# A new order for the later loads and for the work of batches 0 and 1 in a fused attention and feed-forward kernel

## The chip, the cores and the metric

One Trainium2 chip, one core. The metric is device time in microseconds (us). Each execution is listed with its span (first to last instruction) and the mean clock that TensorE was granted. A run of a program on one core carries the state "fast" unless it is more than 1.5% above the fastest of its kernel. The runs were spread over several chips; kernels are compared only with runs of the kernel before on the same chip.

Names used below: PE is TensorE's matmul stream, PEld its weight loads, DVE is VectorE, ACT is ScalarE, POOL is GpSimd, SPq is the queue that issues the loads.

## The reference, cut to what matters

```python
# q, k, v: (8 batches, 8 heads, 576 positions, 64); w_in 512x2048, w_out 2048x512
q_s = softmax(q, axis=-1)                # over the 64 features
k_s = softmax(k, axis=2)                 # over the 576 positions
kv  = einsum('bhsd,bhse->bhde', k_s, v)
x   = einsum('bhsd,bhde->bhse', q_s, kv) # reshaped to 4608 tokens x 512
h   = x @ w_in
out = (h * sigmoid(beta * h)) @ w_out
```

## The kernel before

The 512 main positions of each batch are one chunk of tokens; the last 64 positions of all batches form a ninth. From batch 2 on a loop does the work. Batches 0 and 1, while the weights still arrive, are written out by hand: the program is one long list of small steps, and the place of a step in the list is its place in its engine's queue. The steps that matter here:

```python
def hpe(c, j, kts, tag="h"):      # PE: h block j of chunk c, the 128-row parts kts of w_in
    ...
    nc.tensor.matmul(h[:], w_unit(j, kt), x_of(c)[:, kt, :], start=(kt == 0), stop=(kt == KT - 1))
def th_act(c, j): ...             # ACT: tanh of h
def g_dve(c, j): ...              # DVE: g = (tanh + 1) * h
def mm_b(c, j, sts=None): ...     # PE: 4 matmuls, acc += g x w_out block j
def w_cast(kind, blk, half, eng)  # f32 weights to bf16 on the engine named: G POOL, A ACT, V DVE
def vz_cast(b, j, eng, m=1, part=None)   # f32 v of batch b, head pair j to bf16
def kz_exp(b, j): ...             # ACT: exp of k
def q_exp(b, s) / q_sum / q_mul   # ACT: exp of q; DVE: its sums; DVE: scale by them
def tpe(b, j, tag) / q_ev         # PE: transpose scaled q into a PSUM bank; copy it out
def kvz_mm(b, j) / kvz_norm       # PE: 18 small matmuls k x v; DVE: normalise
def xpe(c, j, tag) / xev          # PE: x = q (kv); copy it out
def warm(n, tag):                 # PE: n matmuls whose result nobody reads
    t = ps.tile([P, 512], F32, tag=bank(tag), bufs=1, name=f"warm{warm_n[0]}")
    ...
```

The loads are issued in this order (cut: the first are batch 0's q, k and v, whose order the change leaves alone):

```python
    w_load("in", 0, 0)
    w_load("in", 0, 3)
    w_load("in", 0, 1)
    w_load("in", 0, 2)
    ...
    w_load("out", 1)
    load_kv(v_st, v, 1, "v_st", [0])
    w_load("in", 3, 0)
    w_load("in", 3, 1)
    load_q(1, 2, 0)
    w_load("out", 2)
    load_q(1, 2, 1)
    load_kv(v_st, v, 1, "v_st", [1])
    load_kv(k_st, k, 1, "k_st", [0])
    ...
```

And three places of the list of work (cuts marked):

```python
    warm(18, tag="b0")
    ...
    warm(13, tag="acc2")
    tpe(0, 0, "acc3")
    ...
    vz_cast(0, 3, G, part=0)
    vz_cast(0, 3, A, part=1)
    kvz_mm(0, 2, "acc1", 2)
    xev(0, 0, A)
    kvz_mm(0, 3)
    ...                                   # 31 us: 
    vz_cast(1, 0, A, part=1)
    th_act(0, 10)
    mm_b(0, 6)
    w_cast("in", 3, 1, A)
    ...                                   # 40 us:
    tpe(1, 0, "b0")
    tpe(1, 1, "b1")
    q_ev(1, 0, A)
    kvz_mm(1, 0, "b3", 2)
    g_dve(0, 14)
    kvz_mm(1, 1)
    q_ev(1, 1, A)
    tpe(1, 3, "b0")
    ...
    kvz_mm(1, 3, "b1", 1)
    vz_cast(1, 2, G, part=0)
    mm_b(0, 14)
    vz_cast(1, 2, A, part=1)
    kvz_norm(1, 3)
    xev(1, 0, A)
    kvz_mm(1, 2, "b0", 1)
    mm_b(0, 15)
```

The softmax here doesn't subtract the row's maximum and nothing guards it: scores larger than these inputs give would overflow.

## Time and profile before

| | before |
|---|---|
| median of 3 runs | 284.43 us (284.4 to 284.81) |
| span of the profiled run | 282.9 us |
| PE busy | 275.2 us, 97% |
| granted clock | 1.000 |

From the page of the kernel before (span, busy time by engine, the clock by fortieths of the span in tenths of full speed, and the chain of work that ended last):

```profile
span 282.9 us, 4278 instructions
...
PE 275.2 (97%) x1653; PEld 130.1 (46%) x1681; DVE 176.5 (62%) x274; ACT 164.9 (58%) x243; POOL 39.6 (14%) x60
...
PEclk9999999999999999999999999999999999999999
...
PE 93%; DMA 3%; SPq 1%; POOL 1%; issue 1%; ACT 0%
```

PE is the bound: it is busy nearly always, at full clock, and the chain that ended last is made of it. So one reads where PE pauses. The timeline of the kernel before, PE alone (start, duration, engine, line, operation, output and inputs, how many merged; in brackets the idle time of the engine ahead of it and what ended it):

```profile
10.51 0.61 PE L273 MATMUL tp<-identity,eq 128*128 128x128 bf16 x8 [0.83 <-DVE eq L243]
...
13.93 0.48 PE L292 MATMUL kv<-va,ek 64*64 64x65 bf16 x18 [0.73 <-POOL va L161]
...
16.30 5.65 PE L425 MATMUL h<-xT,w_in_b 128*128 128x512 bf16 x25
...
39.70 0.61 PE L273 MATMUL tp<-identity,eq 128*128 128x128 bf16 x8
...
45.18 0.48 PE L292 MATMUL kv<-va,ek 64*64 64x65 bf16 x18
...
50.34 1.89 PE L473 MATMUL acc<-w_out_b,g 128*128 128x512 bf16 x8
```

The marks are four: the first transpose of batch 0 (10.51), the start of the long run of w_in matmuls (16.30), the first transpose of batch 1 (39.70) and the first acc matmul of batch 1 (50.34). Two pauses stand in brackets: 0.83 us for DVE's scaled q and 0.73 us for POOL's v cast. A duration of a merged line includes the drain of its last matmul, so pauses of a tenth show only by comparing starts: the 18 kv matmuls at 45.18 start at least 0.1 us after the acc matmuls ahead of them could have ended.

What came before the v cast is in the chain of waits of the kernel before (start, duration, what):

```profile
3.99 8.52 DMA v_st<-in_v_dram
...
12.56 1.31 POOL va L161
13.88 1.13 POOL w_in_b L161 x2
```

The last v load lands at 12.51 us and POOL's cast follows until 13.87.

Waits tell when loads landed. POOL in the timeline of the kernel before, stretches 22 to 33 us and 33 to 46 us:

```profile
28.94 1.04 POOL L161 CAST w_in_b<-w_in 128x1024 bf16<-128x1024 f32 x1 [0.89 <-DMA w_in<-in_moe_w_in_dram]
```

```profile
34.37 1.04 POOL L161 CAST w_out_b<-w_out 128x1024 bf16<-128x1024 f32 x1 [4.39 <-DMA w_out<-in_moe_w_out_dram]
```

Half 0 of block 3 of w_in was waited for until 28.94 us, block 2 of w_out until 34.37. And ACT, same kernel, 19 to 33 us:

```profile
30.57 0.43 ACT L159 CAST va<-v_st 128x256 bf16<-128x256 f32 x1
...
31.45 1.06 ACT L159 CAST w_in_b<-w_in 128x1024 bf16<-128x1024 f32 x1
32.39 1.08 ACT L226 ACTIVATE eq<-q_st 128x1024 bf16<-128x1024 f32 x1
```

ACT casts part of v and the other half of w_in 3 before it starts the exp of batch 1's q at 32.39 us.

### The profile page before, as it was taken

The numbers are of one execution on the slowest core, as the hardware profiler recorded it, in microseconds if no ns is written. First come the engines' busy times: TensorE is split into PE (matmuls) and PEld (weight loads), VectorE is DVE, ScalarE is ACT, GpSimd is POOL, SyncE is SP. The second block draws the span as 40 slices with busy tenths as digits, with TensorE's granted clock in tenths as the row PEclk, the third lists the DMA queues.
The fourth block names the chain that finished last, engine by engine and source line by source line (L and its number), as shares of the span: only waits on it lengthen the run. The fifth ranks groups of instructions, "written<-read, shape, count | busy, mean of one in ns | idle before, by whom it ended". The sixth has DMA issues, their size and how long they took to land.

```text
span 282.9 us, 4278 instructions
## 1 busy us (share of the span) xinstructions
PE 275.2 (97%) x1653; PEld 130.1 (46%) x1681; DVE 176.5 (62%) x274; ACT 164.9 (58%) x243; POOL 39.6 (14%) x60
## 2 busy tenths in 40 slices
PE   8799999999999999999999999999999999999995
PEld 3444454444444544444444444444445444445543
DVE  2864586975487547845785468655964595454361
ACT  2874987954496348644873568346935563554451
POOL 1565235220030003000300030000300000000000
PEclk9999999999999999999999999999999999999999
DMA  7999999929930993099407941599354033005003
GB/s 231 392 393 395 380 392 312 292 44 290 225 151 12 271 272 155 0 227 315 163 5 177 307 158 65 114 233 234 128 88 137 1 148 62 14 0 148 0 2 148
DMA packets 54868, 50.09 MB, mean 177 GB/s; under 512 B 26296, under 2 KB 47040, under 8 KB 54848
## 3 DMA queue, kind: packets, MB, share of 16 engines
q1 hardware_dynamic: 54704, 49.69, 58.7%
q8 instruction: 13, 0.21, 0.3%
q10 hardware_dynamic: 144, 0.13, 0.1%
q14 instruction: 7, 0.06, 0.1%
HBM read 36.71 MB, written 9.44 MB: 163 GB/s over the span
## 4 chain that ended last, share of the span: by engine, by line
PE 93%; DMA 3%; SPq 1%; POOL 1%; issue 1%; ACT 0%
PE h L425 44%; PE acc L473 42%; DMA v_st<-in_v_dram 3%; PE x L373 2%; PE kv L333 2%; PE acc L465 1%; PE kv L292 1%; SPq L122 1%; POOL va L161 0%; POOL w_in_b L161 0%; PE tp L273 0%; PE x L377 0%; SPq L119 0%; SPq L593 0%; SPq L96 0%
## 5 line engine op out<-in xcount | busy, mean ns | idle before, releaser
L435 ACT ACTIVATE th<-h,beta_t 128x512 bf16<-128x512 f32 x144 | 98.2, 688 | 93.4 <-PE h L425 87.2
L439 DVE SCALAR_TENSOR_TENSOR g<-th,h 128x512 bf16<-128x512 bf16 x144 | 97.7, 683 | 84.6 <-ACT th L435 82.7
L425 PE MATMUL h<-xT,w_in_b 128*128 128x512 bf16 x560 | 142.4, 379 | 1.0
L473 PE MATMUL acc<-w_out_b,g 128*128 128x512 bf16 x548 | 138.8, 379 | 0.5 <-issue 0.2
L425 PEld LDWEIGHTS <-w_in_b 128*128 128x128 bf16 x576 | 55.6, 98 | 64.4 <-POOL w_in_b L161 0.4
L473 PEld LDWEIGHTS <-g 128*128 128x128 bf16 x560 | 54.5, 98 | 65.6 <-DVE g L439 0.5
L161 POOL CAST va<-v_st 128x2048 bf16<-128x2048 f32 (+2 forms) x14 | 16.9, 1207 | 149.7 <-DMA v_st<-in_v_dram 149.4
L237 DVE TENSOR_REDUCE rq<-eq 128x16 f32<-128x1024 bf16 x18 | 21.9, 1216 | 7.6 <-ACT eq L226 7.6
L243 DVE TENSOR_TENSOR eq<-eq,rq 128x1024 bf16<-128x1024 bf16 x18 | 22.3, 1239 | 0.1
L226 ACT ACTIVATE eq<-q_st 128x1024 bf16<-128x1024 f32 x16 | 16.1, 1049 | 4.5 <-DMA q_st<-in_q_dram 4.5
L159 ACT CAST xT<-x 128x512 bf16<-128x512 f32 x18 | 10.6, 588 | 6.6 <-PE x L373 5.8
L161 DVE COPY o<-acc 128x512 f32<-128x512 f32 (+1 forms) x19 | 12.1, 670 | 3.4 <-PE acc L473 3.2
L159 ACT COPY o<-acc 128x512 f32<-128x512 f32 (+1 forms) x18 | 9.6, 576 | 7.0 <-PE acc L473 2.9
L161 DVE CAST xT<-x 128x512 bf16<-128x512 f32 x18 | 12.3, 685 | 0.9 <-PE x L373 0.9
L180 ACT ACTIVATE ek<-k_st 128x1024 bf16<-128x1024 f32 x12 | 12.6, 1047 | 0.0
L373 PE MATMUL x<-qsT,kvp 128*128 128x512 bf16 x32 | 11.6, 379 | 0.1
L546 PE MATMUL warm<-kvp 128*128 128x512 bf16 x31 | 8.5, 442 | 1.2 <-DVE kvp L626 1.2
L161 POOL CAST w_in_b<-w_in 128x512 bf16<-128x512 f32 (+1 forms) x12 | 7.5, 650 | 3.0 <-DMA w_in<-in_moe_w_in_dram 2.9
L161 POOL CAST w_out_b<-w_out 128x1024 bf16<-128x1024 f32 x4 | 5.0, 1248 | 7.5 <-DMA w_out<-in_moe_w_out_dram 7.5
L546 PEld LDWEIGHTS <-kvp 128*128 128x128 bf16 x31 | 3.3, 111 | 5.8 <-issue 2.2
L173 ACT ACTIVATE ek<-k_st 128x576 bf16<-128x576 f32 x8 | 5.2, 686 | 1.0 <-DMA k_st<-in_k_dram 1.0
L333 PEld LDWEIGHTS <-ek 128*64 128x64 bf16 x192 | 4.1, 111 | 2.5 <-ACT th L435 2.5
(45 smaller groups left out, 84.6 us busy)
## 6 DMA issues: line engine op xcount, KB each, us to landing
q_st<-in_q_dram SPq DMA_DIRECT2D x7, 1024.0 KB, 6.6
out_dram<-o SPq DMA_DIRECT2D x14, 512.0 KB, 3.4
k_st<-in_k_dram SPq DMA_DIRECT2D x6, 1024.0 KB, 9.5
v_st<-in_v_dram SPq DMA_DIRECT2D x6, 1024.0 KB, 10.6
w_in<-in_moe_w_in_dram SPq DMA_DIRECT2D x6, 512.0 KB, 9.4
v_st<-in_v_dram SPq DMA_DIRECT2D x8, 288.0 KB, 8.5
w_out<-in_moe_w_out_dram SPq DMA_DIRECT2D x4, 512.0 KB, 9.3
w_out<-in_moe_w_out_dram SPq DMA_DIRECT2D x2, 1024.0 KB, 11.2
```

The costliest lines, as they stand in the source:

```text
L159: eng.copy(dst, src)
L161: eng.tensor_copy(dst, src)
L180: nc.scalar.activation(ek[b][:, :, h, :].rearrange("p i h d -> p h i d"), k_st[b][:, h, 0 : R * D].rearrange("p h (i d) -> p h i d", i=R), ...
L226: nc.scalar.activation(eq[b][:, :, s * m : (s + 1) * m, :].rearrange("p i h d -> p h i d"), q_st[b][:, s * m : (s + 1) * m, :].rearrange(" ...
L237: nc.vector.tensor_reduce(rq[b][:, 0, :, h], eq[b][:, :, h, :], axis=AX.X, op=ALU.add)
L243: eng.tensor_tensor(eq[b][:, :, h, :], eq[b][:, :, h, :], rq[b][:, 1, :, h].unsqueeze(3).to_broadcast((P, R, m, D)), ALU.mult,)
L373: nc.tensor.matmul(t[:], kvp[:, c, j, :], qsT[c][:, :, j, :])
L425: nc.tensor.matmul(h[:], w_unit(j, kt), x_of(c)[:, kt, :], start=(kt == 0), stop=(kt == KT - 1),)
L435: nc.scalar.activation(th[:], h_of[c, j][:], ACTF.Tanh, scale=beta_t[:, j : j + 1])
L439: nc.vector.scalar_tensor_tensor(out=g[:], in0=th_of.pop((c, j))[:], scalar=1.0, in1=h_of[c, j][:], op0=ALU.add, op1=ALU.mult)
L473: nc.tensor.matmul(acc[st][:], g[:, ds(st * P, P)], w_out_b[:, j, :], start=(j == 0), stop=(j == NJ - 1),)
L546: nc.tensor.matmul(t[:], kvp[:, B - 1, 0, :], kvp[:, B - 1, :, :].rearrange("p j r -> p (j r)"))
```

## The change

Its words: same loads of batch 0, other order of later loads and of the work of batches 0 and 1 on all engines, worked out for other landing times. No arithmetic is added or removed other than five warm-up matmuls. The core of the diff (cut; bank names that only follow are left out):

```diff
-    HB, AB = ["b3", "b0"], ["b1", "b2"]
+    HB, AB = ["b0", "b1"], ["b2", "b3"]
...
     w_load("in", 0, 0)
-    w_load("in", 0, 3)
     w_load("in", 0, 1)
     w_load("in", 0, 2)
+    w_load("in", 0, 3)
...
     w_load("out", 1)
-    load_kv(v_st, v, 1, "v_st", [0])
+    w_load("in", 3, 1)
     w_load("in", 3, 0)
-    w_load("in", 3, 1)
     load_q(1, 2, 0)
     w_load("out", 2)
     load_q(1, 2, 1)
     load_kv(v_st, v, 1, "v_st", [1])
     load_kv(k_st, k, 1, "k_st", [0])
+    load_kv(v_st, v, 1, "v_st", [0])
     load_kv(k_st, k, 1, "k_st", [1])
     w_load("out", 3, 0)
+    w_load("out", 3, 1)
+    load_kv(k_st, k, 1, "k_st", [2])
+    load_kv(v_st, v, 1, "v_st", [3])
     load_kv(k_st, k, 1, "k_st", [3])
-    w_load("out", 3, 1)
-    load_kv(v_st, v, 1, "v_st", [3])
-    load_kv(k_st, k, 1, "k_st", [2])
...
-    warm(13, tag="acc2")
+    warm(18, tag="acc2")
...                                   # h6 before h7, h9 before h8, h7 after h4 (cut)
...                                   # casts between engines
-    w_castk(0, 2, G)
+    w_castk(0, 2, A)
-    w_cast("out", 0, 1, G)
+    w_cast("out", 0, 1, A)
-    w_castk(2, 2, G)
-    w_castk(2, 3, G)
+    w_castk(2, 2, A)
+    w_castk(2, 3, A)
-    w_cast("in", 3, 1, A)
+    w_cast("in", 3, 1, G)
-    w_cast("out", 3, 0, G)
+    w_cast("out", 3, 0, A)
-    w_cast("out", 3, 1, A)
+    w_cast("out", 3, 1, G)
...                                   # batch 1's attention, as it stands after
     tpe(1, 0, "b0")
     tpe(1, 1, "b1")
+    kvz_mm(1, 0, "b2", 2)
+    q_ev(1, 1, V)
+    kvz_mm(1, 1)
     q_ev(1, 0, A)
+    tpe(1, 3, "b1")
+    kvz_norm(1, 0, 2)
+    tpe(1, 2, "b3")
...
     mm_b(0, 14)
     vz_cast(1, 2, A, part=1)
+    vz_cast(1, 2, G, part=0)
+    kvz_mm(1, 3, "b0", 1)
+    kvz_mm(1, 2, "b1", 1)
     kvz_norm(1, 3)
     mm_b(0, 15)
```

More of the change, by code (lines that the diff above doesn't have):

```diff
@@ L666 @@
     tpe(0, 2, "b3")
-    w_castk(0, 3, G)
+    w_castk(0, 1, G)
     q_ev(0, 3, A)
@@ L671 @@
     xpe(0, 1, "acc3")
-    hpe(0, 2, [0], "b1")
+    hpe(0, 1, [0], "b1")
     q_ev(0, 2, A)
-    w_castk(0, 1, G)
-    hpe(0, 1, [0], "b2")
+    hpe(0, 2, [0], "b2")
     xev(0, 1, V)
     hpe(0, 0, [0], "acc0")
+    w_castk(0, 2, A)
     xpe(0, 3, "acc2")
-    w_castk(0, 2, G)
+    w_castk(0, 3, G)
     xpe(0, 2, "acc1")
     xev(0, 3, V)
+    hpe(0, 0, [1])
+    xev(0, 2, A)
     hpe(0, 1, [1])
-    xev(0, 2, A)
-    hpe(0, 0, [1])
     hpe(0, 3, [1])
@@ L704 @@
     g_dve(0, 1)
-    hpe(0, 6, [0], "b1")
+    hpe(0, 6, [0], "b2")
     hpe(0, 5, [2])
@@ L708 @@
     hpe(0, 5, [3])
-    hpe(0, 7, [0], "b2")
+    hpe(0, 7, [0], "b1")
     th_act(0, 0)
@@ L712 @@
     g_dve(0, 3)
+    hpe(0, 6, [2])
+    hpe(0, 6, [3])
+    th_act(0, 5)
     w_cast("out", 0, 0, G)
     hpe(0, 7, [1])
+    g_dve(0, 0)
     hpe(0, 7, [2])
-    th_act(0, 5)
-    hpe(0, 6, [2])
-    g_dve(0, 0)
-    hpe(0, 6, [3])
-    hpe(0, 7, [3])
+    hpe(0, 4, [0], "b0")
+    th_act(0, 6)
     g_dve(0, 5)
-    th_act(0, 6)
-    hpe(0, 4, [0], "b0")
-    w_cast("out", 0, 1, G)
+    hpe(0, 4, [1])
+    hpe(0, 4, [2])
     mm_b(0, 0)
-    th_act(0, 7)
+    w_cast("out", 0, 1, A)
     g_dve(0, 6)
     mm_b(0, 1)
-    g_dve(0, 7)
     w_castk(2, 0, G)
@@ L733 @@
     mm_b(0, 3)
-    w_castk(2, 2, G)
-    w_castk(2, 3, G)
-    hpe(0, 4, [1])
-    hpe(0, 4, [2])
+    w_castk(2, 2, A)
+    w_castk(2, 3, A)
     hpe(0, 4, [3])
-    hpe(0, 8, [0, 1, 2, 3], "b1")
+    hpe(0, 7, [3])
     th_act(0, 4)
     hpe(0, 9, [0, 1, 2, 3], "b2")
+    th_act(0, 7)
     g_dve(0, 4)
-    th_act(0, 8)
+    hpe(0, 8, [0, 1, 2, 3], "b3")
+    th_act(0, 9)
+    g_dve(0, 7)
     w_cast("out", 1, 0, A)
     hpe(0, 11, [0, 1, 2, 3], "b0")
-    g_dve(0, 8)
-    vz_cast(1, 0, G, part=0)
-    hpe(0, 10, [0, 1, 2, 3], "b1")
-    th_act(0, 9)
-    th_act(0, 11)
-    w_cast("in", 3, 0, G)
-    g_dve(0, 9)
+    g_dve(0, 9)
+    hpe(0, 10, [0, 1, 2, 3], "b1")
+    th_act(0, 8)
+    w_cast("in", 3, 1, G)
+    th_act(0, 11)
+    g_dve(0, 8)
     mm_b(0, 4)
@@ L755 @@
     g_dve(0, 11)
+    w_cast("in", 3, 0, G)
     mm_b(0, 5)
-    vz_cast(1, 0, A, part=1)
     th_act(0, 10)
     mm_b(0, 6)
-    w_cast("in", 3, 1, A)
     g_dve(0, 10)
-    mm_b(0, 7)
     q_exp(1, 0)
@@ L767 @@
     th_act(0, 13)
-    hpe(0, 14, [0, 1, 2, 3], "b2")
-    w_cast("out", 2, 0, A)
-    w_cast("out", 2, 1, G)
-    g_dve(0, 13)
-    hpe(0, 15, [0, 1, 2, 3], "b3")
-    th_act(0, 12)
+    mm_b(0, 7)
+    th_act(0, 12)
+    g_dve(0, 13)
+    w_cast("out", 2, 1, G)
+    w_cast("out", 2, 0, A)
+    hpe(0, 14, [0, 1, 2, 3], "b2")
     q_mul(1, 0)
+    hpe(0, 15, [0, 1, 2, 3], "b0")
     q_exp(1, 1)
+    g_dve(0, 12)
     mm_b(0, 8)
-    g_dve(0, 12)
     vz_cast(1, 1, G)
     th_act(0, 14)
-    mm_b(0, 9)
@@ L781 @@
     q_sum(1, 1)
     th_act(0, 15)
+    mm_b(0, 9)
+    kz_exp(1, 0)
+    vz_cast(1, 0, G, part=0)
     mm_b(0, 10)
-    kz_exp(1, 0)
     g_dve(0, 15)
+    vz_cast(1, 0, A, part=1)
+    kz_exp(1, 1)
+    g_dve(0, 14)
     mm_b(0, 11)
-    kz_exp(1, 1)
     q_mul(1, 1)
-    w_cast("out", 3, 0, G)
     tpe(1, 0, "b0")
+    w_cast("out", 3, 0, A)
     tpe(1, 1, "b1")
+    kvz_mm(1, 0, "b2", 2)
+    q_ev(1, 1, V)
+    kvz_mm(1, 1)
     q_ev(1, 0, A)
-    kvz_mm(1, 0, "b3", 2)
-    g_dve(0, 14)
-    kvz_mm(1, 1)
@@ L796 @@
-    q_ev(1, 1, A)
-    tpe(1, 3, "b0")
-    kz_exp(1, 3)
-    kvz_norm(1, 0, 2)
-    mm_b(0, 12)
-    w_cast("out", 3, 1, A)
-    tpe(1, 2, "b1")
-    xpe(1, 1, "b2")
-    vz_cast(1, 3, G, part=0)
-    q_ev(1, 2, V)
-    xpe(1, 0, "b3")
-    vz_cast(1, 3, A, part=1)
-    mm_b(0, 13)
-    xev(1, 1, V)
-    q_ev(1, 3, A)
-    kz_exp(1, 2)
-    kvz_mm(1, 3, "b1", 1)
-    vz_cast(1, 2, G, part=0)
+    tpe(1, 3, "b1")
+    kvz_norm(1, 0, 2)
+    tpe(1, 2, "b3")
+    w_cast("out", 3, 1, G)
+    mm_b(0, 12)
@@ L814 @@
+    q_ev(1, 2, A)
+    q_ev(1, 3, V)
+    kz_exp(1, 2)
+    xpe(1, 1, "b0")
+    xpe(1, 0, "b1")
+    xev(1, 1, V)
+    mm_b(0, 13)
+    vz_cast(1, 3, A, part=1)
+    vz_cast(1, 3, G, part=0)
+    xev(1, 0, A)
+    kz_exp(1, 3)
     mm_b(0, 14)
     vz_cast(1, 2, A, part=1)
+    vz_cast(1, 2, G, part=0)
+    kvz_mm(1, 3, "b0", 1)
+    kvz_mm(1, 2, "b1", 1)
     kvz_norm(1, 3)
-    xev(1, 0, A)
-    kvz_mm(1, 2, "b0", 1)
     mm_b(0, 15)
     kvz_norm(1, 2)
-    xpe(1, 3, "b1")
+    xpe(1, 3, "b0")
@@ L822 @@
     store(0, 0)
-    xpe(1, 2, "b0")
+    hpe(1, 0, [0], "b2")
     xev(1, 3, V)
-    hpe(1, 0, [0], "b2")
     hpe(1, 0, [1])
+    xpe(1, 2, "b1")
+    hpe(1, 1, [0], "b3")
+    store(0, 1)
     xev(1, 2, A)
-    hpe(1, 2, [0], "b3")
-    store(0, 1)
+    hpe(1, 1, [1])
+    hpe(1, 2, [0], "b0")
     hpe(1, 2, [1])
-    hpe(1, 1, [0], "b1")
     hpe(1, 0, [2])
+    store(0, 2)
     hpe(1, 0, [3])
-    store(0, 2)
-    hpe(1, 1, [1])
     hpe(1, 1, [2])
+    store(0, 3)
     th_act(1, 0)
-    store(0, 3)
@@ L839 @@
     hpe(1, 1, [3])
     hpe(1, 2, [2])
+    hpe(1, 2, [3])
     th_act(1, 1)
-    hpe(1, 2, [3])
+    hpe(1, 3, [0], "b1")
     g_dve(1, 0)
-    hpe(1, 3, [0], "b0")
     hpe(1, 3, [1])
+    hpe(1, 3, [2])
     th_act(1, 2)
-    hpe(1, 3, [2])
+    hpe(1, 3, [3])
     g_dve(1, 1)
-    hpe(1, 3, [3])
     mm_b(1, 0)
```

## The prediction

> **What bounds the kernel now.** TensorE. The page gives PE 275.2 of 282.9 us busy (97%), clock 1.00; the chain that ended last is 93% PE. The stage table has PE busy 33.72 of 34.04 us between 16.3 and 50.34 us. By hand: 145 matmuls of 512 columns at a pitch of 0.216 us (16 take 3.45 us), 16 transposes at 0.067 and 72 kv matmuls at 0.02 make 33.8 us. The Trainium skill ("TensorE: Matmul & The Clock Gate", Part 1) gives 215.7 ns per warm 512-column matmul; the trace agrees. So the reordered stretch holds some 0.2 us of stalls to win. Before 16 us PE waits 0.83 us for the first scaled q and 0.73 us for the v cast (chain: v load landed at 12.51 us, GpSimd cast until 13.88). The loads behind both are untouched.
>
> **What changes.** No arithmetic is removed. Added: 5 warm-up matmuls (1.1 us), which fill the 0.83 us hole and delay the first transpose by 0.1 to 0.2 us; the v wait absorbs that. Moved: casts between GpSimd and ScalarE; h6 before h7, h9 before h8, h7 after h4; PSUM banks (a consistent renaming); batch 1's first v load (288 KB), to seven loads later.
>
> **Loads.** By the slices the queues run full at about 390 GB/s until 44 us, so landings are running sums of sizes. Before (GpSimd's waits): v1[0] 27.6, w_in 3 28.9 and 30.3, w_out 2 34.4, w_out 3 39.4 and 41.5, last v piece 43.7 us. After, estimated: w_in 3 28.2/29.5, w_out 2 33.6, v1[0] 37.2, w_out 3 39.3/40.7, last piece 43.7. Nothing lands after its use.
>
> **Where stalls may appear,** from queues added up with trace durations (tanh 0.64 back to back, ScalarE cast 1.04, g 0.64, DVE sum and reciprocal 1.45, scale 1.2):
> 1. From 25.9 us ScalarE has five tanh and two w_out casts before the second half of w_out 1 is ready, about 31.2 us; PE wants it at about 31.1: 0.1 to 0.4 us.
> 2. DVE ends batch 1's second q scale at about 40.9 us, then evicts transpose 1 (0.42 us) before transpose 3 can reuse its bank: PE waits 0.2 to 0.4 us. Before, ScalarE did that copy and PE did not wait.
> 3. ScalarE's last exp and cast of batch 1 end at about 44.9/45.3 us, just when PE asks: 0 to 0.3 us; in exchange the short waits of before (0.4 us in all, 43.8 to 45.8) shrink.
> Net: batch 1's first acc matmul starts at 50.4 to 50.9 us against 50.34. From there both kernels are the same PE-limited stream; what is lost stays lost.
>
> **Prediction.** About +0.35 us: **284.8 us**, 8 in 10 between **284.2 and 286.2**. Faster by over 2% 0.01, within 2% 0.97, slower by over 2% 0.02. A gain beyond 0.3 us is not there to be had.
>
> **What would show it.** Right: first transpose within 0.3 us of 10.5; w_in matmuls running without pause from near 16.3; short waits (below 0.5 us) on a ScalarE w_out cast near 31 us and on DVE near 41 us; identical pace after 51 us. Wrong: batch 1's acc matmuls starting before 50.1 or after 51.5 us, or another pace later.
>
> **What would make it wrong.** A GpSimd cast stretched by VectorE (one took 1.87 us, others 1.04) that lands on PE's path; the load queue running dry near 20 us; a chain of ScalarE, VectorE and bank waits in 31 to 46 us that feeds on itself, so that small slips add up to 2 us.

## The result, and the profile after

| | before | after |
|---|---|---|
| median (lowest to highest), 4 runs each | 284.53 us (284.4 to 284.81) | 285.20 us (284.64 to 285.9) |
| ratio after to before | | 1.0023 (95% interval 0.9999 to 1.0048) |
| clocks of the four runs after | | 0.994, 0.998, 1.000, 1.000 |
| span of the profiled run | 282.9 us | 284.1 us |

A ratio is the mean time of one kernel's fast runs over that of the other's of the same rounds, so it is not quite the ratio of the medians.

(The four runs before are the three of the first table and one more.) The same within noise, as predicted, with a time inside the range. The page of the kernel after, the same lines:

```profile
span 284.1 us, 4292 instructions
...
PE 277.1 (98%) x1658; PEld 131.0 (46%) x1686; DVE 176.6 (62%) x275; ACT 165.7 (58%) x245; POOL 37.4 (13%) x57
...
PEclk9979999999999999999999999999999999999999
...
PE 93%; DMA 3%; SPq 1%; issue 1%; POOL 0%; ACT 0%
```

One digit of the clock is a 7: near the third fortieth, 14 to 21 us, the clock fell. The timeline of PE after:

```profile
10.49 0.61 PE L273 MATMUL tp<-identity,eq 128*128 128x128 bf16 x8
...
13.90 0.48 PE L292 MATMUL kv<-va,ek 64*64 64x65 bf16 x18 [0.72 <-POOL va L161]
...
15.98 1.49 PE L425 MATMUL h<-xT,w_in_b 128*128 128x512 bf16 x3
...
17.95 5.78 PE L425 MATMUL h<-xT,w_in_b 128*128 128x512 bf16 x26
...
41.26 0.61 PE L273 MATMUL tp<-identity,eq 128*128 128x128 bf16 x8
...
46.08 0.77 PE L292 MATMUL kv<-va,ek 64*64 64x65 bf16 x36
...
51.53 1.89 PE L473 MATMUL acc<-w_out_b,g 128*128 128x512 bf16 x8
```

Before 14 us nothing has moved: the first transpose at 10.49 (10.51 before), the v wait until 13.90. Then three w_in matmuls take 1.49 us instead of 0.81, and the long run starts at 17.95 us instead of 16.30. That is 1.65 us lost, in a stretch where the change moves only casts and the order of single w_in matmuls. After it the kernel is *faster*: from the start of the long run to the first acc matmul of batch 1 it takes 51.53 - 17.95 = 33.58 us where the kernel before took 50.34 - 16.30 = 34.04, and of these 0.46 us, 0.37 lie behind the first transpose of batch 1 (10.27 us against 10.64). From there to the end of the span are 232.57 us against 232.56: the same stream.

The busy table in stretches (the stretch, its length, busy time and count of each engine, then the clock, the DMA share and GB/s), kernel before:

```profile
core 0: us, PE busy (x) PEld busy (x) DVE busy (x) ACT busy (x) POOL busy (x), PEclk, DMA share, GB/s
...
10.40:14.30 3.90, 2.97 (x83) 2.35 (x83) 3.65 (x9) 3.46 (x8) 3.65 (x5) 1.00 1.05 390
14.30:17.70 3.40, 3.35 (x28) 1.83 (x23) 2.13 (x5) 1.66 (x3) 2.89 (x6) 1.00 1.05 389
```

and kernel after:

```profile
10.40:14.30 3.90, 3.08 (x84) 2.35 (x83) 3.63 (x9) 3.43 (x8) 3.64 (x5) 1.00 1.05 384
14.30:17.70 3.40, 3.18 (x19) 1.74 (x16) 1.44 (x4) 1.59 (x3) 2.23 (x5) 0.51 1.04 367
```

After, the clock was 0.51 from 14.3 to 17.7 us; read in stretches of 0.2 us, the half clock runs from 14.37 to 17.78, which is 3.41 us. The loss of 1.65 us is about half of that.

So the profiled run holds two things, a stretch at half clock and a gain of 0.46 us, and at least two of the four runs after had a clock of 1.000 and were still no faster than before. Something else must eat the gain. Three theories went to the chip:

- CLOCK: the half-clock stretch hits some runs of either kernel. It is what makes single runs of the changed kernel long.
- WARM, later LATE-START: the five added warm-up matmuls cost time.
- ORDER: the new order costs or gains; and if it gains, which part does.

### The profile page after: what moved, and what is told of

It reads as the page before. It is cut to its first block, busy times and chain, and to the rows that moved or that the text cites. A ratio compares the mean times of both kernels' runs of the same rounds, so it can differ in the third digit from the quotient of the medians.

```text
span 284.1 us, 4292 instructions
## 1 busy us (share of the span) xinstructions
PE 277.1 (98%) x1658; PEld 131.0 (46%) x1686; DVE 176.6 (62%) x275; ACT 165.7 (58%) x245; POOL 37.4 (13%) x57
## 4 chain that ended last, share of the span: by engine, by line
PE 93%; DMA 3%; SPq 1%; issue 1%; POOL 0%; ACT 0%
PE h L425 44%; PE acc L473 42%; DMA v_st<-in_v_dram 3%; PE x L373 3%; PE kv L333 2%; PE acc L465 1%; PE kv L292 1%; SPq L122 1%; PE tp L273 1%; POOL va L161 0%; PE x L377 0%; ACT qsT L159 0%; SPq L119 0%; SPq L96 0%; ACT o L159 0%
## 5 line engine op out<-in xcount | busy, mean ns | idle before, releaser
L161 POOL CAST va<-v_st 128x2048 bf16<-128x2048 f32 (+2 forms) x14 | 17.9, 1279 | 148.4 <-DMA v_st<-in_v_dram 148.1
L159 ACT CAST xT<-x 128x512 bf16<-128x512 f32 x18 | 10.5, 586 | 8.0 <-PE x L373 7.2
L373 PE MATMUL x<-qsT,kvp 128*128 128x512 bf16 x32 | 12.3, 397 | 0.3 <-ACT qsT L159 0.2
L546 PE MATMUL warm<-kvp 128*128 128x512 bf16 x36 | 9.4, 427 | 1.2 <-DVE kvp L626 1.2
L161 POOL CAST w_in_b<-w_in 128x512 bf16<-128x512 f32 (+1 forms) x10 | 6.8, 698 | 8.3 <-DMA w_in<-in_moe_w_in_dram 8.3
L159 ACT CAST w_out_b<-w_out 128x1024 bf16<-128x1024 f32 x5 | 5.3, 1053 | 0.0
## 6 DMA issues: line engine op xcount, KB each, us to landing
v_st<-in_v_dram SPq DMA_DIRECT2D x6, 1024.0 KB, 10.4
```

The costliest lines, as they stand in the source:

```text
L159: eng.copy(dst, src)
L161: eng.tensor_copy(dst, src)
L373: nc.tensor.matmul(t[:], kvp[:, c, j, :], qsT[c][:, :, j, :])
L546: nc.tensor.matmul(t[:], kvp[:, B - 1, 0, :], kvp[:, B - 1, :, :].rearrange("p j r -> p (j r)"))
```

## The experiments

Twelve kernels, in three groups of four, each group on one chip beside 9 to 11 runs of the kernel before. Medians in us:

| run | what it is | before, same chip | this | ratio (95%) |
|---|---|---|---|---|
| a_again | changed kernel, unaltered | 284.89 | 285.09 | 1.0000 (0.9983 to 1.0018) |
| b_again | kernel before, unaltered | 284.89 | 284.81 | 0.9996 (0.9983 to 1.0009) |
| a_warm13 | changed, 13 warm-ups | 284.89 | 284.50 | 0.9982 (0.9969 to 0.9996) |
| b_warm18 | before, 18 warm-ups | 284.89 | 285.24 | 1.0008 (0.9994 to 1.0021) |
| b_newtail | before, new order from batch 1's attention on | 284.82 | 284.75 | 0.9999 (0.9988 to 1.0011) |
| a13_oldtail | a_warm13, old order from there on | 284.82 | 284.83 | 0.9999 (0.9987 to 1.0011) |
| a_warm23 | changed, 23 warm-ups | 284.82 | 286.60 | 1.0053 (1.0030 to 1.0077) |
| b_warm0 | before, second warm-up run left out | 284.82 | 286.82 | 1.0067 (1.0045 to 1.0089) |
| a13_oldloads | a_warm13, old order of loads | 284.86 | 285.23 | 1.0011 (0.9997 to 1.0025) |
| b_newloads | before, new order of loads | 284.86 | 293.06 | 1.0285 (1.0271 to 1.0299) |
| a13_fill | a_warm13 and 2 filler matmuls | 284.86 | 284.40 | 0.9986 (0.9973 to 0.9998) |
| a13_va | a_warm13, a v cast moved to ACT | 284.86 | 284.44 | 0.9985 (0.9972 to 0.9997) |

### a_again: the changed kernel once more

No edit.

> The changed kernel once more, unaltered. Three theories. CLOCK: the whole difference is one stretch of about 3.4 us at half clock near 14 to 18 us, which hits some runs and not others; then runs split: those with mean granted clock 1.000 last 284.4 to 285.0 us (equal to before within 0.3 us), those with 0.994 to 0.998 last 285.3 to 286.0, about 0.28 us more for each 0.001 of clock. ORDER: the new order itself costs; then even the runs at clock 1.000 lie 0.4 us or more above before. WARM: the 5 added warm-up matmuls bring the half-clock stretch about; then it appears here in about half of the runs, and not in the version with 13.

Measured: 284.21, 285.77, 285.12, 284.59, 285.19 and 285.07 us at clocks 0.999, 0.994, 1.000, 0.999, 0.999 and 1.000. One run of six fell to 0.994 and is the longest, as CLOCK says. But the runs at 0.999 and 1.000 still spread over 1 us, of which CLOCK says nothing. The profiled run was the fastest; its PE timeline:

```profile
10.97 0.61 PE L273 MATMUL tp<-identity,eq 128*128 128x128 bf16 x8
...
16.24 5.77 PE L425 MATMUL h<-xT,w_in_b 128*128 128x512 bf16 x26
...
39.55 0.61 PE L273 MATMUL tp<-identity,eq 128*128 128x128 bf16 x8
...
49.82 1.89 PE L473 MATMUL acc<-w_out_b,g 128*128 128x512 bf16 x8
```

Without the half-clock stretch the new order again takes 49.82 - 16.24 = 33.58 us and again 10.27 from the first transpose of batch 1. Its first transpose came 0.5 us late (10.97) and the long run did not (16.24). ORDER as a cost is refuted: the order gains. The gain that belongs to the order is the 0.37 us behind the first transpose of batch 1. The stretch from the start of the long run to that transpose took 23.31 us here, but also in two profiles of the old order (b_warm0 and b_warm18), and 23.53 to 23.86 in the changed order with 13 warm-ups (a_warm13, a13_fill, a13_va): it varies with how long PE waits near 20 us for w_in 1.

### b_again: the kernel before, against itself

No edit.

> The kernel before, unaltered, against itself. CLOCK: it has the same weakly busy stretch of TensorE from 10.5 to 14.3 us, so it should fall to half clock in some runs too: at least one of the runs with clock below 0.999 and a time of 285.3 to 286.0 us; the others 284.3 to 284.8. ORDER or WARM: all runs at clock 1.000 and 284.3 to 284.8 us. Ratio to itself 1.000 within 0.002 either way.

Measured: 284.73 to 285.14 us, no run below 0.998. But of the 11 runs of the kernel before that ran beside it, two lasted 286.08 and 286.03 us at clock 0.993, against 284.68 to 285.04 for the other nine. So the kernel before falls into the half-clock stretch too; the expected slow runs appeared in its twin. Its profile reads 10.63 us from the first transpose of batch 1 to the first acc matmul (50.77 - 40.14), so the 10.64 of before was no accident.

### a_warm13: the warm-ups undone

```diff
-    warm(18, tag="acc2")
+    warm(13, tag="acc2")
```

> The changed kernel with the second run of warm-up matmuls back at 13. CLOCK: the half-clock stretch comes as often as with 18 or more often, since TensorE is idle 0.8 us longer before 10.5 us; runs at clock 1.000 last 284.4 to 285.0 us as with 18. WARM: all runs at clock 1.000. ORDER: no change from the version with 18 in the runs at clock 1.000, 0.4 us or more above before.

Measured: 284.40 to 284.76 us, six runs within 0.36 us, 0.39 us below before on the same chip. So with 13 warm-ups the new order *is* a small gain, and the five added matmuls take it back. The difference of the means of a_again and a_warm13 is 284.99 - 284.53 = 0.46 us; without a_again's one half-clock run it is 0.31 us, and with runs that spread over 1 us that is not clear of noise by itself. The two profiles don't show it either, since a_again's is its fastest run: batch 1's first acc matmul starts at 49.82 us there and at 50.14 in a_warm13. What shows the cost is the next two runs. (The ratio of 0.9982 is flattered by the two half-clock runs of the kernel before; the medians give 0.9986.) All clocks were 0.998 or more: that fewer warm-ups make the half clock as frequent or more frequent, as CLOCK expected, did not show in six runs.

### b_warm18: the warm-ups alone

```diff
-    warm(13, tag="acc2")
+    warm(18, tag="acc2")
```

> The kernel before with 18 instead of 13 in the second run of warm-up matmuls. CLOCK: as before, with the first transpose still at about 10.5 us; runs at clock 1.000 last 284.3 to 284.8 us, and half-clock runs are as rare as or rarer than with 13. WARM: about half of the runs at clock 0.994 to 0.998 and 285.3 to 286.0 us. ORDER: equal to before, all runs at 284.3 to 284.8 us.

Measured: 284.83 to 285.52 us, median 285.24, 0.43 above b_again. The expectation of the first transpose "still at about 10.5" failed. The PE timeline of this run:

```profile
11.42 0.61 PE L273 MATMUL tp<-identity,eq 128*128 128x128 bf16 x8
...
16.70 5.56 PE L425 MATMUL h<-xT,w_in_b 128*128 128x512 bf16 x25
```

The warm-ups stand ahead of the transposes in PE's queue. The first ten or so run at a pitch of 0.43 us, the later ones at 0.216. (The busy table gives a clock of 1.00 in the first 4 us of every profile all the same: its record of the clock starts only when the clock first rises.) How many are slow differs between executions: the profiles show 7 to 12 pauses of 0.2 to 0.3 us between their weight loads. With 13 the first transpose came between 10.42 and 10.77 us in all profiles, about when the scaled q is ready; with 18 it came at 10.49, 10.97 and 11.42. No run of this kernel had a clock below 0.998, so WARM in its first form (the warm-ups bring the half clock on) found no support; what the trace shows is a late start, 0.4 us at the long run. It shows a second loss too: PE waits 0.27 us at 41.58 us for DVE's second scale of q, which took 2.07 us here against 1.21 before, beside a cast on POOL that had started 0.04 us ahead of it. So the 0.43 us is not all late start.

### a_warm23: the suspected cost doubled

```diff
-    warm(18, tag="acc2")
+    warm(23, tag="acc2")
```

> The changed kernel with 23 in the second run of warm-up matmuls instead of 18 (or 13). LATE-START theory: the warm-ups cost when they end after the scaled q is ready at about 10.4 us; the 0.73 us wait for the v cast absorbs up to about 0.5 us, the rest is lost. Five more add 1.08 us to a start that is already late, so the first transpose comes at 11.6 to 12.5 us, the first long w_in run at 17.0 to 17.8 instead of 16.3, and the median is 0.8 to 1.2 us above that with 18 (285.1), 1.4 to 1.8 above that with 13 (284.5). CLOCK (the warm-ups only change how often the half-clock stretch comes): median within 0.3 us of the version with 18.

Measured: median 286.60 us, 1.5 above a_again and 2.1 above a_warm13 (these two on another chip), runs from 284.92 to 287.36, all but one at clock 1.000. PE's timeline:

```profile
12.52 0.61 PE L273 MATMUL tp<-identity,eq 128*128 128x128 bf16 x8
...
17.80 5.77 PE L425 MATMUL h<-xT,w_in_b 128*128 128x512 bf16 x26
```

The first transpose comes 2.0 us late and the long run 1.5 us. Together with a_again (0.5 late, nothing lost) and b_warm18 (0.9 late, 0.4 lost) this gives the rule of this kernel: the v wait absorbs 0.5 us of a late start, and the rest reaches the long run one for one. Some of it is won back where PE would have waited for w_in 1: the first acc matmuls start at 23.41 us here against 22.17 in a_warm13, 1.24 us later and not 1.52. LATE-START holds. The median rose a little more than expected (0.8 to 1.2). The profiled run also waited twice, 0.4 us each, for the transposing DMA of a later batch; that is a part of it. Why these waits come is open; b_warm0's profile has one too (0.38 us).

### b_warm0: the second warm-up run left out

```diff
-    warm(13, tag="acc2")
```

> The kernel before without the second run of 13 warm-up matmuls: TensorE is idle from about 7 to 10.5 us, a whole 3.4 us. CLOCK: weak activity over such a stretch brings the half clock on (the Trainium skill, TensorE: Matmul & The Clock Gate, Part 1, says a window of about 3.4 us and states that an idle one takes the clock to half); then every run has clock 0.990 to 0.995, one or two stretches of 3.4 us at half clock between 10 and 18 us, and the median is 1.2 to 3 us above before. If the warm-ups do nothing for the clock: clock 1.000 and the time of before within 0.2 us, since the first transpose still waits for the scaled q at 10.5 us.

Measured: five runs of 286.73 to 287.53 us at clocks 0.986 to 0.988, and one, the profiled one, of 285.04 at 0.999. In it PE stood still for 2.69 us ahead of the first transpose and the clock did not fall. So the warm-ups are worth about 2 us in most runs, and whether the clock falls is a matter of chance in each execution. The Trainium skill, page "TensorE: Matmul & The Clock Gate", Part 1, says that the clock follows an activity window of about 3.4 us which runs freely and does not start with the kernel; that fits both the length of 3.4 us in the trace after and one lucky run in six. The kept traces show the window: their clock changes only at whole multiples of 3.413 us after its first rise (after: full for 10.24 us, which is three, then half for one; b_newloads: full for nine, half for two). That first rise comes between 4.1 and 6.4 us in the nine traces where it can be placed, so the same weak stretch is cut differently in each execution. How busy PE must be in a window is not shown: it was busy for 2.60 us in the window before the fall in the trace after, and for 1.50 us in one of this run's (6.21 to 9.63 us), after which the clock did not fall.

### b_newtail: the new order from batch 1's attention on, alone

```diff
     g_dve(0, 15)
+    g_dve(0, 14)
     mm_b(0, 11)
     kz_exp(1, 1)
     q_mul(1, 1)
-    w_cast("out", 3, 0, G)
     tpe(1, 0, "b0")
+    w_cast("out", 3, 0, A)
     tpe(1, 1, "b1")
... (from here on the changed list, its banks, and its order of the last five loads)
```

> The kernel before, with the changed order only from batch 1's attention on (after acc j=11), with the banks and the last five loads that go with it. TAIL theory: the gain of the new order sits there, since that stretch (first transpose of batch 1 to first acc matmul of batch 1) took 10.63 and 10.64 us in the profiles of the old order against 10.27 in all three of the new; then it is 10.2 to 10.4 us here and the kernel is 0.25 to 0.45 us below before. Rival, HEAD: the gain comes from the order of 16 to 31 us (w_in and w_out casts); then this kernel equals before within 0.15 us.

Measured: 284.61 to 285.01 us, ratio 0.9999. Neither TAIL nor its expected 10.2 to 10.4 us: the PE timeline has 50.38 - 39.71 = 10.67 us, and a new wait.

```profile
39.71 0.61 PE L273 MATMUL tp<-identity,eq 128*128 128x128 bf16 x8
...
41.36 0.61 PE L273 MATMUL tp<-identity,eq 128*128 128x128 bf16 x8 [0.33 <-DVE qsT L161]
...
50.38 1.89 PE L473 MATMUL acc<-w_out_b,g 128*128 128x512 bf16 x8
```

PE waits 0.33 us at 41.36 for DVE's copy of transpose 1. This is the wait that the prediction expected of the changed kernel (0.2 to 0.4 us near 41 us). It exists, but only when the new tail stands behind the old head: there DVE starts the second scale of q at 39.75 us, just after the transposes begin; in a_again it started at 38.88, 0.67 us ahead of them. DVE in b_newtail, then in a_again:

```profile
39.75 1.22 DVE L243 TENSOR_TENSOR eq<-eq,rq 128x1024 bf16<-128x1024 bf16 x1
```

```profile
38.88 1.22 DVE L243 TENSOR_TENSOR eq<-eq,rq 128x1024 bf16<-128x1024 bf16 x1
```

By starts this wait cost 0.41 us (the second transposes come 1.65 us after the first, in a_again 1.24), and 10.67 less 0.41 is the 10.27 of the new order.

### a13_oldtail: the complement

```diff
... (a_warm13 up to q_mul(1, 1), then the old list, its banks, and its order of the last five loads)
     q_mul(1, 1)
+    w_cast("out", 3, 0, G)
     tpe(1, 0, "b0")
-    w_cast("out", 3, 0, A)
     tpe(1, 1, "b1")
-    kvz_mm(1, 0, "b2", 2)
-    q_ev(1, 1, V)
+    q_ev(1, 0, A)
+    kvz_mm(1, 0, "b3", 2)
...
```

> The complement: the changed order with 13 warm-up matmuls, but from batch 1's attention on the old order, banks and last loads. TAIL: that stretch takes 10.5 to 10.8 us and the kernel equals before within 0.15 us, 0.3 to 0.4 us above the changed order with 13 warm-ups (284.5). HEAD: it keeps the gain, 0.25 to 0.45 us below before.

Measured: 284.68 to 284.91 us, ratio 0.9999; 50.31 - 39.79 = 10.52 us in the tail. As TAIL expected. With b_newtail: the new head alone gains nothing, the new tail alone gains nothing, both together gain 0.4 us (measured on two other chips, against the kernel before there). The old tail splits the last kv matmuls into two groups, each behind its own acc matmuls and each starting 0.1 us late; the new tail merges them into one group with one such gap. The trace puts the old gaps down to ACT copies, but these had ended 0.3 us earlier, and the gap of the new tail is the same size, so its cause is open. The new tail needs DVE to be early, which only the new head makes.

### a13_oldloads: the new work with the old loads

```diff
     w_load("in", 0, 0)
+    w_load("in", 0, 3)
     w_load("in", 0, 1)
     w_load("in", 0, 2)
-    w_load("in", 0, 3)
... (the whole list of loads as before; work as changed, 13 warm-ups)
```

> The changed work order with 13 warm-up matmuls, but the old order of loads. PAIR theory: the gain of 0.3 us needs the new loads too, because the first v load of batch 1, moved later, lets w_out 2 land at 33.7 instead of 34.4 us, so the ScalarE cast and exp behind it and the second q scale on VectorE come 0.5 to 0.8 us earlier; with the old loads TensorE waits 0.2 to 0.5 us near 41 us for VectorE's copy of transpose 1, as in the kernel before with the new tail, and up to 0.5 us for the w_in 3 casts, now both on GpSimd, near 32 us: median equal to before or up to 0.7 us above. Rival, WORK: the work order alone makes the gain; then 284.4 to 284.6, 0.25 to 0.45 us below before.

Measured: 285.00 to 285.39 us, 0.37 above before. WORK, that the order of work alone gains, is refuted. PAIR was right in outcome and half right in place. PE near 32 us:

```profile
32.92 1.90 PE L425 MATMUL h<-xT,w_in_b 128*128 128x512 bf16 x8 [0.26 <-POOL w_in_b L161]
```

and POOL, same run:

```profile
30.84 2.03 POOL L161 CAST w_in_b<-w_in 128x1024 bf16<-128x1024 f32 x2 [6.23 <-DMA w_in<-in_moe_w_in_dram]
```

Both w_in 3 casts are now POOL's, one behind the other; with the old loads they start at 30.84 us and PE waits for them; by starts PE lost 0.42 us there (from the acc matmuls ahead to the w_in matmuls are 3.01 us, in a13_fill 2.59). The wait expected near 41 us did not come: with PE itself late, DVE was in time, and the tail took 51.00 - 40.70 = 10.30 us.

This gives the chain. Moving 288 KB of v behind w_in 3 lets the first half of w_in 3 to be loaded land about 0.7 us earlier (waited for until 28.24 us in the trace after, against 28.94), POOL can then cast both halves in time, and ACT is freed of one of them, 1.06 us, and of a piece of v, 0.43. POOL in the trace after and ACT in a_again:

```profile
28.24 1.04 POOL L161 CAST w_in_b<-w_in 128x1024 bf16<-128x1024 f32 x1 [4.11 <-DMA w_in<-in_moe_w_in_dram]
```

```profile
31.08 1.06 ACT L226 ACTIVATE eq<-q_st 128x1024 bf16<-128x1024 f32 x1
```

It starts the exp of batch 1's q at 31.08 us against 32.39 before; DVE's sums and scale follow, and the tail finds them done. (The run with the old loads also has a wait of 0.41 us near 20 us for w_in 1. b_again has one of 0.35 there, and before none that shows, so it need not be theirs. But it is a part of the 0.83 us by which this run's median lies above a13_fill's on the same chip; 0.42 us of that is shown to come from the loads. This run puts back the whole old list, with the two halves of w_in 3 swapped too; which of its moves counts was not tested one by one.)

### b_newloads: the new loads with the old work

```diff
     w_load("in", 0, 0)
-    w_load("in", 0, 3)
     w_load("in", 0, 1)
     w_load("in", 0, 2)
+    w_load("in", 0, 3)
... (the whole list of loads as changed; work as before)
```

> The kernel before with the new order of loads only. Both engines' casts of batch 1's first v piece stand early in the old work order, ahead of both w_in 3 casts, and that piece now lands at about 37 us: GpSimd and ScalarE wait for it, TensorE waits about 5 to 7 us for w_in 3 near 33 us, and the kernel takes 289 to 293 us. If landing order mattered little at this size (0.75 us of data moved), it would be within 1 us of before.

Measured: 292.45 to 293.36 us, all four runs at clock 0.988. POOL and PE in its timeline, and the busy table from 39 to 43 us:

```profile
37.45 0.46 POOL L161 CAST va<-v_st 128x320 bf16<-128x320 f32 x1 [11.93 <-DMA v_st<-in_v_dram]
```

```profile
38.95 5.67 PE L425 MATMUL h<-xT,w_in_b 128*128 128x512 bf16 x16 [5.87 <-POOL w_in_b L161]
```

```profile
39.00:43.00 4.00, 4.00 (x10) 1.39 (x11) 2.76 (x5) 3.35 (x5) 2.94 (x4) 0.50 1.06 380
```

POOL waits 11.93 us for a piece of v with the w_in 3 cast behind it in its queue. PE's wait is 5.87 us, as expected, but the time is at or above the upper end of what was expected, because the wait costs more than itself. The clock falls to 0.50 while PE still waits, at 36.30 us, and rises at 43.13, two stretches of 3.41 us later; the 16 matmuls after the wait, which take 3.45 us elsewhere, take 44.46 - 38.95 = 5.51. 5.87 + 2.06 is 7.9 of the 8.2 us. Here the clock fell in every run, and the wait is longer than the 3.4 us that the skill's page names.

### a13_fill: filler in the v wait

```diff
     xev(0, 0, A)
+    warm(2, tag="b1")
     kvz_mm(0, 3)
```

> The changed kernel with 13 warm-up matmuls and 2 filler matmuls in TensorE's 0.73 us wait for the v cast at 13.2 us. They fit in the wait (0.43 us), so the time is that of 13 warm-ups without them, 284.4 to 284.6, within 0.15 us. CLOCK: no run with clock below 0.996, as the weakly busy stretch is busier; few runs, so this alone settles nothing. If they delay the v matmuls, up to 0.3 us is lost.

Measured: 284.29 to 284.62 us, no clock below 0.998. They fit. The PE timeline of this run, for comparison with the next:

```profile
16.21 5.99 PE L425 MATMUL h<-xT,w_in_b 128*128 128x512 bf16 x26
22.05 3.62 PE L473 MATMUL acc<-w_out_b,g 128*128 128x512 bf16 x16
```

### a13_va: the v cast moved

```diff
-    vz_cast(0, 3, G, part=0)
-    vz_cast(0, 3, A, part=1)
+    vz_cast(0, 3, A)
```

> The changed kernel with 13 warm-up matmuls and the last v cast of batch 0 wholly on ScalarE. In the profiles GpSimd's part of it, 320 columns, took 1.3 us where the same cast later took 0.46, with VectorE scaling q beside it. LOAD-BOUND theory: the matmuls behind it come 0.4 to 0.6 us earlier and the wait of 0.73 us goes, but TensorE then waits longer for the second half of w_in 1, which lands at about 19 us, so 0.5 to 0.8 us of waiting on its casts appear near 19.5 us and the median stays at 284.4 to 284.6. Rival, CAST-BOUND: the start is bound by the cast; then the whole gain stays and the median is 284.0 to 284.2.

Measured: 284.31 to 284.51 us, the same as a13_fill. CAST-BOUND is refuted. PE:

```profile
13.46 0.48 PE L292 MATMUL kv<-va,ek 64*64 64x65 bf16 x18 [0.16 <-ACT va L159]
...
15.96 3.59 PE L425 MATMUL h<-xT,w_in_b 128*128 128x512 bf16 x15
19.74 2.55 PE L425 MATMUL h<-xT,w_in_b 128*128 128x512 bf16 x11 [0.20 <-POOL w_in_b L161]
22.12 3.62 PE L473 MATMUL acc<-w_out_b,g 128*128 128x512 bf16 x16
```

The kv matmuls come at 13.46 us instead of 13.90 and the long run at 15.96 instead of 16.28. But the run then breaks at 19.74 us on the cast of the second half of w_in 1, which landed at 19.01 us by the chain of waits of this run, and the acc matmuls start at 22.12 against 22.05. The start of this kernel is bound by when w_in 1 lands; in this run, what was won ahead of that was slack. (Why the POOL cast took 1.3 us: the skill's page "SBUF — State Buffer", section "SBUF: two separate sides", calls the port pair that GpSimd and VectorE share an exclusive lock. In the trace before the cast started at 12.56 us and ended at 13.87, just after DVE's scale of q that ran from 12.33 to 13.56; the same shape took 0.46 us elsewhere. That agrees with the page. The traces show it from both sides later on: before, DVE's scale started first (39.16 us) and POOL's cast beside it took 1.87 us instead of 1.04; in b_warm18 the cast started first (39.41) and the scale took 2.07 instead of 1.21. No run here takes the neighbour away and leaves the rest.)

### What the runs say of the clock

Runs at clock 0.994 or below, near 286 us: 2 of 37 recorded runs of the kernel before (b_again included; four of these by their times alone, since no clock is on record for them), 2 of 10 of the changed kernel, and none of the 43 runs of a_warm13, b_warm18, b_newtail, a13_oldtail, a13_va, a13_fill, a13_oldloads and a_warm23. Both kernels do it. Whether the change makes it more frequent stays open: the counts are too small. A mean clock of 0.998 or 0.999 is another matter: in the six profiles that have one, the half clock lies at the end, after PE's last matmul (in a_again from 281.76 us of 282.41), and costs nothing.

## Why the prediction was right or wrong

- **The time.** 284.8 us was predicted, range 284.2 to 286.2; measured 285.20, ratio 1.0023 and, in the second set of six runs, 1.0000. Right, and "within 2%" was right. But that is luck: of its terms the warm-ups, put at nothing, cost time, and the reordering, put at a loss, gained, and the two nearly cancel.
- **"The v wait absorbs that" (warm-ups cost nothing).** Mis-sized. The prediction put the delay of the first transpose at 0.1 to 0.2 us. It was 0, 0.5 and 0.9 us in three profiles with 18 warm-ups, because the number of slow warm-ups varies. The v wait absorbs 0.5 us of it, not 0.7. What the five warm-ups cost is 0.46 us on average in the changed kernel (a_again against a_warm13; 0.31 without the half-clock run) and 0.43 in the median of the old one (b_warm18 against b_again, where a part is a later wait for DVE).
- **"Where stalls may appear", net +0.1 to +0.5 us.** Wrong in sign. None of the three waits shows above 0.1 us in a_again, the profile of the changed kernel without the half clock; the reordered work took 33.58 us against 34.04. The failed step is the adding-up of queues, which came out late at each of its three places. In a_again the second half of w_out 1 was cast at 30.61 us where 31.2 had been summed, and PE asked for it at 30.92 (the start of its acc matmuls, 29.19, and eight of them). Q's second scale ended at 40.10 where 40.9 had been summed. The last exp and cast ended at 43.98 and 44.45 where 44.9 and 45.3 had been summed. The wait on the copy of transpose 1 is a real one, 0.33 us, but of another kernel (b_newtail).
- **"The reordered stretch holds some 0.2 us of stalls to win."** Mis-sized: it held 0.46, of which 0.37 lie in batch 1's attention; the other 0.09 the old order also saves in some runs. The pitches multiplied by counts gave 33.8 us for a stretch that the changed order does in 33.58 (one matmul of 512 columns too many was counted: the trace of a_again lists 144). With PE 97% busy such a sum must be good to 0.5% to rule a gain out.
- **"From there both kernels are the same PE-limited stream."** Right: 232.56 and 232.57 us in the two first profiles, 232.5 to 232.6 in nearly all. Three profiles show 0.3 to 1.0 more there; for two of them the trace names a wait of 0.4 us, once or twice, for a transposing DMA.
- **What would show it.** The first transpose was within 0.3 us of 10.5, as predicted. "W_in matmuls running without pause from near 16.3" failed in the profiled run (17.95) and held in a_again (16.24). "Wrong if batch 1's acc matmuls start after 51.5" was met by a hair (51.53), and the cause was none of those listed: the half-clock stretch, which the prediction did not consider at all.
- **"The load queue running dry", "a GpSimd cast stretched onto PE's path"** were listed as risks and did not happen in the changed kernel.
- **Best version.** The changed order with 13 warm-ups. In three variants, on two chips, it is 0.14 to 0.18% below the kernel before, each interval just clear of 1. The changed kernel as given is not.

## What to carry to other kernels

Warm-up work on an in-order engine is a queue entry like any other: size it by the latest time at which it can end, not by its mean, because its own speed varies between executions. An order of work and an order of loads are one object: each half of this change alone gained nothing or lost up to 8 us, and only the pair gained 0.4. And when a kernel is 97% busy on its bound, compare runs by their granted clock, and see where in the span it fell, before reading anything into a difference of a microsecond.

## What the Trainium skill lacked or had wrong

- "TensorE: Matmul & The Clock Gate", Part 1, gives half clock after an idle window and full clock after a busy one, but not how much activity counts as busy. Here the clock fell to half for 3.41 us right after a window of 3.41 us in which PE was recorded busy for 2.60 us, and did not fall in b_warm0's profile after one with 1.50, so the busy time that the profile shows does not decide it alone.
- The same page advises not to fit to a count of slow matmuls because the penalty is below 1% of a span. That holds (7 to 12 slow warm-ups, each 0.21 us longer, are at most 2.6 us of 285), but the advice to warm up comes without a warning that the warm-ups hold up the real work behind them: five too many moved a median by as much as the whole gain of a reordering.
- The pitch of 215.7 ns for a warm matmul of 512 columns and the window of about 3.4 us agree with the traces (16 in 3.45 us; half clock from 14.37 to 17.78 us).
